# Attention beside a Fourier mix on one core: the place of a unit's negated maximum, the columns of the value matmuls, and two smaller edits

## The chip, the cores and the metric

The kernel runs on one core of one Trainium2 chip. The metric is the device time of one execution in microseconds (us), the median of several runs. All matrices are float32; TensorE reads most of them in the float32r form.

## The reference

The input x has 2048 rows of 640. Two branches are computed from it and mixed by a gate per row:

```python
q, k, v = split(x @ wqkv)                       # 32 heads of 20
p = softmax(q @ k.T * 20**-0.5)                 # 2048 x 2048 for each head
a = (p @ v, heads side by side) @ wo            # 640 x 640
b = dft_seq_re @ (x @ dft_hid_re.T) - dft_seq_im @ (x @ dft_hid_im.T)
g = sigmoid((x * gate_w).sum(-1))
out = g * a + (1 - g) * b
```

## The kernel before

Heads are taken in 16 pairs, and each pair in two halves of the queries, so attention has 32 **units** of 1024 queries by 2048 keys for two heads. PE computes the scores of a unit twice. The first time (`s_mm`, kind "m") queries lie on the output rows, and DVE takes the maximum of every 512 keys (L199) as soon as the scores stand in PSUM. The second time (kind "e", L950) keys lie on the output rows, with the negated maximum added through two extra rows of the query stack, and ACT takes the exponential (L952) into the tile `p`. The maximum work runs 41 steps ahead of the exponentials (`LEAD`); a unit is 32 steps, each with two "m" and two "e" matmuls.

When the last maximum of a unit is done, `max_nm` reduces its 128x64 block maxima to 128x16 negated ones on DVE (`nm`, L213). `max_chain` transposes them on PE (L231), splits the transpose in two on DVE (L115, L116) and sends the rows to the query stack by DMA.

The value product is `av_step`: for one key tile of 128 keys four matmuls (two heads, two query blocks), each with its own strip of 32 output rows of one PSUM bank `av`. The stationary operand is a piece of `v`, the tile of a pair's values, in which a head has 21 columns (20 values and a column of ones that gives the softmax's sum). A piece of 32 columns reaches into the next head's columns, and past the end for the last one, for which `v` has 16 more columns, set to zero on POOL. In the trace each of these float32 matmuls counts as two.

Under the attention runs the Fourier branch, piece by piece: first the products with the hidden matrices (`hid_tile`, L379), then seven products with sums of sequence matrices (`dft_step`, L636), last the output projection (`out_tile`, L743). The sequence matrices come by DMA as `raw` tiles (three buffers in turn), are combined on POOL (L516), cast on ACT (L113), and the rest is split off on POOL (L116) into a `part` tile (two buffers). In the seventh product `dft_step` also loads the five row blocks of the output weights `wo` through `raw` tiles, and POOL splits each in four instructions.

The order of all this is written out by hand. A string in `ORDERS` gives, for one **cycle**, the order of "e" and "m" scores, of fills "F" with Fourier matmuls, and at its end a burst "B": the value matmuls of the key tiles that are done, three of them in the Fourier stage (`k == 1`) and two elsewhere. There, too, the burst holds the unit's `max_nm` and, ahead of its last key tile, `max_chain`. Instructions stand on each engine in the order in which they are called. Score tiles share five PSUM banks in turn (`bank`), so a score matmul waits until the reader of the score five before it is done.

Ahead of all this the projections of q and k (`qk_tile`) run with weights in `part` tiles: the rounded part and the rest of 640 columns each, made by `w_tiles`, 4096 bytes apart. The values' projection (`v_pair`) gathers its results in `v` tiles.

Of the kernel before, what the change touches and what calls it, by code (L numbers as in the profile page):

```python
# [11 lines left out]
F32 = mybir.dt.float32  # L12
# [7 lines left out]
P = 128  # L20
# [3 lines left out]
DH = 20  # L24
ND = D // P
NS = S // P
NP = H // 2
HE = D // 2
VW = 2 * (DH + 1)
# [48 lines left out]
def mix_kernel(ctx: ExitStack, tc: tile.TileContext, xa, wqk, wb, cdft, wo, out):  # L78
# [59 lines left out]
    def part_tile():  # L138
        return work.tile([P, 2, 1024], R, name="part", bufs=2)

    def w_tiles():
        w = part_tile()
        return [w[:, z, : ND * P].rearrange("p (d c) -> p d c", d=ND) for z in range(2)]

    def v_tile():
        return work.tile([P, NS * VW + 16], F32, name="v", bufs=2)

# [27 lines left out]
        p, u = VISITS[n]  # L177
        return third["q"] if p == 14 else qst[place(p)][:, u * (S // 2) : (u + 1) * (S // 2)]

    mx, nms, ends = {}, {}, []  # L180
    now, later = [-1], {}

    def at_step(i, fn):
# [17 lines left out]
    def s_end(i):  # L201
        n, s = divmod(i, 32)
        if n < NU and s == 31:
            if now[0] < 0:
                max_nm(n)
            else:
                ends.append(n)
        if s == 1 and 0 < n <= NU and now[0] < 0:
            max_chain(n - 1)

    def max_nm(n):
        nms[n] = small.tile([P, 16], F32, name="nm", bufs=2)
        dve.tensor_reduce(nms[n], mx.pop(n).rearrange("p h q c -> p (h q) c"), axis=AX.X, op=ALU.max, negate=True)  # L213
# [47 lines left out]
    vts = {}  # L261

    def load_v(n):
        p = VISITS[n][0]
        if n and VISITS[n - 1][0] == p:
            vts[n] = vts[n - 1]
            return
        vts[n] = v_tile()
        pool.memset(vts[n][:, NS * VW :], 0.0)
        sp.dma_start(vts[n][:, : NS * VW].rearrange("p (s e) -> p s e", s=NS), v_scr[p])  # L270

    def load_x(t):
        for d in range(0, ND, 2):
# [75 lines left out]
            three(ps[:, :n], x[:, 0, d, cs], x[:, 1, d, cs], w[:, 0, d, :n], w[:, 1, d, :n], d == 0, d == ND - 1)  # L349

    def v_pair(hf, s):
        vst = v_tile()[:, : NS * VW].rearrange("p (a k e) -> p a k e", a=NP // 2, k=2)
        pool.memset(vst, 1.0)
        for k in range(2):
            ps = bank()
            mm_b(hf, s + k, ps, HE + 2 * hf)
            act.activation(
                vst[:, :, k, :].rearrange("p a (h e) -> p a h e", h=2)[:, :, :, :DH],
                ps[:, :HE].rearrange("p (a h e) -> p a h e", h=2, e=DH), AF.Copy)
            if hf:  # L360
                act.activation(logit[:, s + k : s + k + 1], ps[:, HE : HE + 1], AF.Copy)
        stores.append((
            v_scr[hf * (NP // 2) : (hf + 1) * (NP // 2), :, s : s + 2, :].rearrange("a p k e -> p a (k e)"),
            vst.rearrange("p a k e -> p a (k e)")))
        flush(1)
# [181 lines left out]
    def av_step(i, n, kt, split_unit):  # L547
        v = vts[n]
        if split_unit:
            next_av()  # L550
        t, c0 = av["tile"], kt * VW
        pp = [pts.pop((n, kt, qc)) for qc in range(2)]
        for qc in range(2):
            for h in range(2):
                j = 2 * qc + h
                pe.matmul(t[32 * j : 32 * j + 32, :], v[:, c0 + h * (DH + 1) : c0 + h * (DH + 1) + 32],  # L556
                          pp[qc][:, h, :], start=kt == 0, stop=kt == NS - 1)
        if kt == NS - 1:
            unit_end(i, n)

# [52 lines left out]
    def dft_step(g):  # L613
        n, t, s = g // NS // HT, g // NS % HT, g % NS
        if s == 0:
            new_y(0), new_y(1)
            outs[n, t] = []
        if s % 8 == 0 and g // 8 + 3 < 2 * UNITS:
            cfin.append(load_c(g // 8 + 3))
        if s % 8 == 2 and g // 8 + 2 < 2 * UNITS:  # L620
            cfin[0][0]()
        if s == 8:
            for _, th, hf in PRODUCTS[n][2]:
                tt = th * HT + t
                y = None
                if (tt, hf) in signs:
                    y = apool[0].tile([P, HE], F32, name="yt", bufs=4)
                    sp.dma_start(y, y_scr[tt, :, hf * HE : (hf + 1) * HE])
                outs[n, t].append(y)
        c = cparts[g // 8]  # L630
        cs = slice((s % 8) * P, (s % 8 + 1) * P)
        a = at[n % 2, s]
        for z, (cz, az) in enumerate(((0, 0), (0, 1), (1, 0))):
            for h in range(2):
                r = slice(64 * h, 64 * h + 64)
                pe.matmul(yp[h][:, :HE], c[r, cz, cs], a[r, az], start=s == 0 and z == 0, stop=s == NS - 1 and z == 2)  # L636
            if z < 2:
                yield
        w = g % (HT * NS) - 16
        if n + 1 == len(PRODUCTS) and w >= 0:  # L640
            d, r = divmod(w, 8)
            if r == 0 and d < ND:
                wos[d] = raw_tile()[:, :D]
                sp.dma_start(wos[d], wo[:, d])
            if r == 5 and d < ND:
                raw = wos.pop(d)
                for h in range(2):
                    wos[d, h] = a_tile(1, 2 * d + h)
                    split(wos[d, h][:, 0], wos[d, h][:, 1], raw[:, h * HE : (h + 1) * HE], pool, pool)
        if s == NS - 1:  # L650
            m = apool[1].tile([P, HE], F32, name="m", bufs=2)
            y0, y1 = yp[0][:, :HE], yp[1][:, :HE]

            def read():
                act.activation(m, y0, AF.Copy)
                dve.tensor_tensor(m, y1, m, op=ALU.add)

            extras.append((now[0], read))
            for out_, y in zip(PRODUCTS[n][2], outs.pop((n, t))):
                extras.append((now[0] + 3, functools.partial(finish_y, out_, t, m, y)))  # L660
        yield
# [163 lines left out]
    start = 4 * HID  # L825
# [129 lines left out]

    def burst(c):
        for n in ends:
            max_nm(n)
        k, _, i = phase(c)
        steps = 6 if k == 1 else 4  # L960
        run_extras(steps - 2)
        if k == 1:
            run_casts()
        for kt in range(i // 2, (i + steps) // 2):
            if k == 1 and ends and kt == (i + steps) // 2 - 1:
                max_chain(ends.pop(0))
            av_step(now[0], kt // NS, kt % NS, kt % NS == 0 and kt > i // 2)
        while ends:
            max_chain(ends.pop(0))
        if c in (HID - NS - 1, HID - 1):  # L970
            next_pool()
# [4 lines left out]
    for c in range(len(goals)):  # L976
        k, base, i = phase(c)
        order, *heads_ = ORDERS[k]
        first = dict(zip("em", heads_))
        for x, kind in enumerate(order):  # L980
            if kind == "F":
                fill(c)
            elif kind == "B":
                burst(c)
            else:
                score(kind)
            if k == 1 and x == len(order) // 2:
                run_loads(c - HID)
# [114 lines left out]
```

## Time and profile before

| | |
|---|---|
| runs | 1876.40, 1879.57 and 1880.56 us; median 1879.57 |
| the profiled execution | 1879.31 us; its span 1877.5 us, mean granted clock 0.998 |
| PE, PE's weight loads, DVE, ACT, POOL busy | 99%, 73%, 74%, 72%, 53% of the span |
| value matmuls (L556) | 4096, 485.3 us busy |
| negated maxima (L213) and their transposes (L231) | 32 of each; 6.8 and 8.9 us busy |

A row of the timeline or of a group names the line, the engine and the operation, then output and inputs by the program's names, then shapes; PEld is PE's weight load, which runs beside matmuls. In square brackets stands how long the engine had been empty before the row, and whose end it waited for last. Rows of the waits give total us, times and the longest. A matmul's own duration overlaps with its neighbours', so what counts on PE is the distance between starts.

### The profile page before, as it was taken

Reading aid. Unit: us, or ns where it says so; the run is one execution under the profiler, and the core shown is the slowest. Engines: PE = TensorE matmul, PEld = TensorE weight load, DVE = VectorE, ACT = ScalarE, POOL = GpSimd, SP = SyncE. Lnnn points to the kernel's source line nnn. Section 1 sums busy time; section 2 is a strip of 40 time slices with the busy share of each in tenths; the row PEclk is TensorE's granted clock in tenths of the full one; section 3 lists DMA queues with packets and bytes.
Section 4 is the critical chain, followed back from the end, with each engine's and each line's share of the span. In section 5 each row is a group of like instructions: output and inputs, shape, how many; then the busy total and the mean of one; then the engine's idle time right before and its main releaser. Section 6 shows DMA issues by size and latency. Waiting matters only on the chain.

```text
span 1877.5 us, 44813 instructions
## 1 busy us (share of the span) xinstructions
PE 1858.4 (99%) x17606; PEld 1372.2 (73%) x17606; DVE 1380.5 (74%) x2309; ACT 1355.7 (72%) x2645; POOL 1002.0 (53%) x851
## 2 busy tenths in 40 slices
PE   9999999999999999999999999999999999999998
PEld 8988777676767777777777777777777777776666
DVE  3043457887877888888888888888888888888853
ACT  4222257787877787788788788778878877778885
POOL 3334432121146676344678688655668767545544
PEclk9999999999999999999999999999999999999999
DMA  6754341222134673536567576646375856531233
GB/s 228 164 146 148 136 129 55 78 64 68 53 102 135 211 217 127 155 116 192 183 191 232 162 248 198 186 136 182 127 231 186 244 174 194 172 90 52 83 97 108
DMA packets 178771, 281.61 MB, mean 150 GB/s; under 512 B 44811, under 2 KB 113547, under 8 KB 178559
## 3 DMA queue, kind: packets, MB, share of 16 engines
q1 hardware_dynamic: 177599, 276.77, 48.4%
q0 software_dynamic: 960, 1.97, 0.6%
q8 instruction: 138, 2.26, 0.5%
q14 instruction: 74, 0.61, 0.1%
HBM read 214.61 MB, written 63.52 MB: 148 GB/s over the span
## 4 chain that ended last, share of the span: by engine, by line
PE 95%; DVE 3%; issue 0%; DMA 0%; POOL 0%; ACT 0%; SPq 0%; POOLq 0%; ACTq 0%; DVEq 0%
PE ps L556 23%; PE yp L636 19%; PE ps L950 17%; PE ps L197 14%; PE yp L379 7%; PE ps L119 4%; PE ps L120 4%; PE ps L121 4%; PE yp L743 3%; DVE mx L199 3%; PE ps L231 0%; DMA p<-in_xa 0%; DVE nm L213 0%; PE ps L1037 0%; POOL raw L516 0%
## 5 line engine op out<-in xcount | busy, mean ns | idle before, releaser
L199 DVE TENSOR_REDUCE mx<-ps 128x1 f32<-128x512 f32 x2048 | 1280.7, 683 | 327.7 <-PE ps L197 297.5
L952 ACT ACTIVATE p<-ps 128x512 f32<-128x512 f32 x2048 | 1054.1, 611 | 298.9 <-PE ps L197 193.8
L950 PE MATMUL ps<-qst,kst 62*128 62x512 f32 x1920 | 728.2, 407 | 0.1
L197 PE MATMUL ps<-kst,qst 60*128 60x512 f32 x1920 | 668.1, 411 | 0.0
L636 PE MATMUL yp<-x,part 64*128 64x320 f32 x5376 | 629.2, 307 | 0.0
L636 PEld LDWEIGHTS yp<-x,part 64*128 64x128 f32 x5376 | 606.0, 186 | 5.8 <-ACT raw L389 0.4
L556 PE MATMUL ps<-p,v 128*32 128x512 f32 x4096 | 485.3, 597 | 0.0
L116 POOL TENSOR_TENSOR part<-raw,part 128x1024 fp32r<-128x1024 f32 (+1 forms) x128 | 287.2, 2244 | 345.2 <-ACT part L113 329.5
L950 PEld LDWEIGHTS ps<-qst,kst 62*128 62x128 f32 x1920 | 341.7, 185 | 155.0 <-DVE mx L199 85.5
L197 PEld LDWEIGHTS ps<-kst,qst 60*128 60x128 f32 x1920 | 318.7, 184 | 12.5 <-issue 4.2
L556 PEld LDWEIGHTS ps<-p,v 128*32 128x32 f32 x4096 | 110.8, 109 | 233.0 <-issue 225.1
L379 PE MATMUL yp<-wb,x 64*128 64x320 f32 x1920 | 224.5, 307 | 0.0
L379 PEld LDWEIGHTS yp<-wb,x 64*128 64x128 f32 x1920 | 210.1, 186 | 6.4
L390 POOL TENSOR_TENSOR raw<-raw 128x320 f32<-128x320 f32 x64 | 55.7, 870 | 268.1 <-ACT raw L389 215.0
L516 POOL TENSOR_TENSOR raw<-raw,raw 128x1024 f32<-128x1024 f32 x77 | 185.2, 2405 | 0.1
L113 ACT ACTIVATE part<-raw 128x1024 fp32r<-128x1024 f32 (+2 forms) x121 | 123.4, 1020 | 6.0 <-POOL raw L516 4.1
L743 PE MATMUL yp<-x,part 64*128 64x320 f32 x768 | 102.6, 309 | 0.0
L339 ACT ACTIVATE p<-ps 128x512 f32<-128x512 f32 x40 | 23.8, 597 | 104.1 <-PE ps L121 101.1
L116 POOL TENSOR_TENSOR x<-araw,x 128x320 fp32r<-128x320 f32 x112 | 97.9, 882 | 1.3
L743 PEld LDWEIGHTS yp<-x,part 64*128 64x128 f32 x768 | 92.0, 186 | 1.0
L119 PE MATMUL ps<-x,part 128*128 128x512 f32 x200 | 81.4, 407 | 1.5 <-ACT x L113 1.3
L120 PE MATMUL ps<-x,part 128*128 128x512 f32 x200 | 80.0, 400 | 0.2 <-DVE x L116 0.2
(102 smaller groups left out, 1363.1 us busy)
## 6 DMA issues: line engine op xcount, KB each, us to landing
raw<-in_cdft SPq DMA_DIRECT2D x192, 512.0 KB
araw<-a_scr SPq DMA_DIRECT2D x192, 160.0 KB
qk_scr<-p SPq DMA_DIRECT2D x40, 512.0 KB
kst<-qk_scr SPq DMA_DIRECT2D x84, 160.0 KB
qst<-qk_scr SPq DMA_DIRECT2D x84, 160.0 KB
yt<-y_scr SPq DMA_DIRECT2D x80, 160.0 KB
a_scr<-raw SPq DMA_DIRECT2D x64, 160.0 KB
y_scr<-yt SPq DMA_DIRECT2D x64, 160.0 KB
```

Source lines behind the costliest of these rows:

```text
L116: e2.tensor_tensor(dst2, src, f32(dst1), op=ALU.subtract)
L119: pe.matmul(ps, st1, mv1, start=first, stop=False)
L120: pe.matmul(ps, st1, mv2, start=False, stop=False)
L197: pe.matmul(ps, q[b : b + KROWS, qt * P : (qt + 1) * P], k[b : b + KROWS, kc * 512 : (kc + 1) * 512], start=True, stop=True)
L199: return lambda: dve.tensor_reduce(mx[n][:, h, qt, kc : kc + 1], ps, axis=AX.X, op=ALU.max)
L379: pe.matmul(yp[h][:, :HE], x[r, xz, d, cs], w[r, wz, d, :HE], start=d == 0 and z == 0, stop=d == ND - 1 and z == 2)
L516: pool.tensor_tensor(raws[0], raws[0], raws[1], op=ALU.add if PRODUCTS[n][0][1][0] > 0 else ALU.subtract)
L556: pe.matmul(t[32 * j : 32 * j + 32, :], v[:, c0 + h * (DH + 1) : c0 + h * (DH + 1) + 32], pp[qc][:, h, :], start=kt == 0, stop=kt == NS - 1)
L636: pe.matmul(yp[h][:, :HE], c[r, cz, cs], a[r, az], start=s == 0 and z == 0, stop=s == NS - 1 and z == 2)
L743: pe.matmul(yp[h][:, :HE], o[oz][r], wos[d, hf][r, wz], start=d == 0 and z == 0, stop=end)
L950: pe.matmul(pt, k[b : b + KROWS + 2, kt * P : (kt + 1) * P], q[b : b + KROWS + 2, qc * 512 : (qc + 1) * 512], start=True, stop=True)
L952: act.activation(pts[n, kt, qc][:, h], pt, AF.Exp, scale=float(DH) ** -0.5)
```

## The change

Four things change. `max_nm` is called right behind a unit's last maximum in the Fourier stage, and the burst calls it only where that has not been done. The value matmuls take 21 columns for all key tiles but a unit's first, which keeps 32 so that the whole strip is written once; with it the pad of `v` and its memset go. `w_tiles` lays the two parts one behind the other, 2560 bytes apart. The output weights' loads and splits come every 16 steps of the seventh product in place of every 8.

```diff
     def w_tiles():
-        w = part_tile()
-        return [w[:, z, : ND * P].rearrange("p (d c) -> p d c", d=ND) for z in range(2)]
+        w = part_tile().rearrange("p z c -> p (z c)")[:, : 2 * ND * P].rearrange("p (z d c) -> p z d c", z=2, d=ND)
+        return [w[:, z] for z in range(2)]
 
     def v_tile():
-        return work.tile([P, NS * VW + 16], F32, name="v", bufs=2)
+        return work.tile([P, NS * VW], F32, name="v", bufs=2)
...
             if now[0] < 0:
                 max_nm(n)
             else:
+                if early:
+                    max_nm(n)
                 ends.append(n)
...
         vts[n] = v_tile()
-        pool.memset(vts[n][:, NS * VW :], 0.0)
-        sp.dma_start(vts[n][:, : NS * VW].rearrange("p (s e) -> p s e", s=NS), v_scr[p])
+        sp.dma_start(vts[n].rearrange("p (s e) -> p s e", s=NS), v_scr[p])
...
                 j = 2 * qc + h
-                pe.matmul(t[32 * j : 32 * j + 32, :], v[:, c0 + h * (DH + 1) : c0 + h * (DH + 1) + 32],
-                          pp[qc][:, h, :], start=kt == 0, stop=kt == NS - 1)
+                r, m = c0 + h * (DH + 1), DH + 1 if kt else 32
+                pe.matmul(t[32 * j : 32 * j + m, :], v[:, r : r + m], pp[qc][:, h, :], start=kt == 0, stop=kt == NS - 1)
...
         if n + 1 == len(PRODUCTS) and w >= 0:
-            d, r = divmod(w, 8)
+            d, r = divmod(w, 16)
...
     def burst(c):
         for n in ends:
-            max_nm(n)
+            if n not in nms:
+                max_nm(n)
...
         first = dict(zip("em", heads_))
+        early[:] = [c] if k == 1 else []
```

PE and ACT keep their order instruction for instruction. On DVE 14 of the 32 reductions `nm` move. The first place is the end of the Fourier stage's first cycle with a unit's end in it; `mx_7821` holds that unit's maxima, `mx_8697` the next unit's, and `ps0` to `ps5` are the banks. Before:

```order
L199 TENSOR_REDUCE mx_7821<-ps0_8667 128x1
L199 TENSOR_REDUCE mx_7821<-ps2_8677 128x1
L199 TENSOR_REDUCE mx_8697<-ps4_8698 128x1
L199 TENSOR_REDUCE mx_8697<-ps0_8701 128x1
L199 TENSOR_REDUCE mx_8697<-ps2_8707 128x1
L199 TENSOR_REDUCE mx_8697<-ps3_8710 128x1
L213 TENSOR_REDUCE nm_8713<-mx_7821 128x16
```

And now (the numbers of the tiles differ from build to build):

```order
L199 TENSOR_REDUCE mx_7817<-ps0_8662 128x1
L199 TENSOR_REDUCE mx_7817<-ps2_8672 128x1
L215 TENSOR_REDUCE nm_8675<-mx_7817 128x16
L199 TENSOR_REDUCE mx_8694<-ps4_8695 128x1
L199 TENSOR_REDUCE mx_8694<-ps0_8698 128x1
L199 TENSOR_REDUCE mx_8694<-ps2_8704 128x1
L199 TENSOR_REDUCE mx_8694<-ps3_8707 128x1
```

The reduction moves ahead of four maxima of the next unit; so it does in seven units. In seven others the unit's last maximum comes earlier in its cycle. DVE before, two units on, where `mx_9579` is the unit's:

```order
L199 TENSOR_REDUCE mx_9579<-ps1_10433 128x1
L199 TENSOR_REDUCE mx_10443<-ps5_10444 128x1
L199 TENSOR_REDUCE mx_10443<-ps3_10455 128x1
L199 TENSOR_REDUCE mx_10443<-ps5_10474 128x1
L199 TENSOR_REDUCE mx_10443<-ps3_10484 128x1
L199 TENSOR_REDUCE mx_10443<-ps2_10503 128x1
L199 TENSOR_REDUCE mx_10443<-ps5_10506 128x1
L199 TENSOR_REDUCE mx_10443<-ps3_10512 128x1
L199 TENSOR_REDUCE mx_10443<-ps1_10515 128x1
L213 TENSOR_REDUCE nm_10518<-mx_9579 128x16
```

And now:

```order
L199 TENSOR_REDUCE mx_9574<-ps1_10427 128x1
L215 TENSOR_REDUCE nm_10430<-mx_9574 128x16
L199 TENSOR_REDUCE mx_10439<-ps5_10440 128x1
L199 TENSOR_REDUCE mx_10439<-ps3_10451 128x1
L199 TENSOR_REDUCE mx_10439<-ps5_10470 128x1
L199 TENSOR_REDUCE mx_10439<-ps3_10480 128x1
```

Here it moves ahead of eight, of which the first two free banks (`ps5`, `ps3`) that scores of the same cycle write again (`ps5_10474`, `ps3_10484` before).

On POOL the output weights' splits (L115 and L116 on `x` from `raw`) stand elsewhere in the seventh product. Before, from the end of a unit's normalisation (L588) to the fifth split:

```order
L588 TENSOR_TENSOR o<-o,rb 128x512
L115 CAST x_24259<-raw 128x320
L116 TENSOR_TENSOR x_24259<-raw,x_24259 128x320
L115 CAST x_24259<-raw 128x320
L116 TENSOR_TENSOR x_24259<-raw,x_24259 128x320
L116 TENSOR_TENSOR part<-raw,part 128x1024
L269 MEMSET v 128x16
L516 TENSOR_TENSOR raw<-raw,raw_24664 128x1024
L115 CAST x_23778<-raw 128x320
L116 TENSOR_TENSOR x_23778<-raw,x_23778 128x320
L115 CAST x_23778<-raw 128x320
L116 TENSOR_TENSOR x_23778<-raw,x_23778 128x320
```

And now:

```order
L589 TENSOR_TENSOR o<-o,rb 128x512
L116 TENSOR_TENSOR part<-raw,part 128x1024
L517 TENSOR_TENSOR raw<-raw,raw_24644 128x1024
L115 CAST x_24245<-raw 128x320
L116 TENSOR_TENSOR x_24245<-raw,x_24245 128x320
L115 CAST x_24245<-raw 128x320
L116 TENSOR_TENSOR x_24245<-raw,x_24245 128x320
```

The four instructions ahead of the subtraction into `part` are gone (they were the fourth split), and at the fifth's place stands the third one; the last two follow 16 and 32 steps later. On SP the loads of these two move with them.

More of the change, by code (lines that the diff above doesn't have):

```diff
@@ L178, in q_unit @@
         return third["q"] if p == 14 else qst[place(p)][:, u * (S // 2) : (u + 1) * (S // 2)]
-    mx, nms, ends = {}, {}, []
+    mx, nms, ends, early = {}, {}, [], []
     now, later = [-1], {}
@@ L351, in v_pair @@
     def v_pair(hf, s):
-        vst = v_tile()[:, : NS * VW].rearrange("p (a k e) -> p a k e", a=NP // 2, k=2)
+        vst = v_tile().rearrange("p (a k e) -> p a k e", a=NP // 2, k=2)
         pool.memset(vst, 1.0)
```

## The prediction

> **What bounds the kernel now.** I read the page first: the span, the engines' busy time and the chain that ended last.
>
> ```profile
> span 1877.5 us, 44813 instructions
> PE 1858.4 (99%) x17606; PEld 1372.2 (73%) x17606; DVE 1380.5 (74%) x2309; ACT 1355.7 (72%) x2645; POOL 1002.0 (53%) x851
> PE 95%; DVE 3%; issue 0%; DMA 0%; POOL 0%; ACT 0%; SPq 0%; POOLq 0%; ACTq 0%; DVEq 0%
> ```
>
> The end is set by PE. DVE, ACT and POOL have a quarter to a half of the span free, so an edit is worth what it takes out of PE's own row: a wait there, or a matmul that starts sooner. I therefore looked next in the waits for what stops PE's weight loads, and found one row that the change touches.
>
> ```profile
> PEld ps L231 <- DVE nm L213: 36.3, 31, 1.4
> ```
>
> L231 is the transpose of a unit's 16 negated maxima, L213 the reduction that makes them. Not all of the 36.3 us is a wait: a transpose never follows value matmuls at once. The timeline shows the floor, in the hidden-product stage, and then the same spot in the Fourier stage for the three kinds of unit there.
>
> ```profile
> 293.72 0.21 DVE L213 TENSOR_REDUCE nm<-mx 128x16 f32<-128x64 f32 x1
> 294.51 0.09 PEld L231 LDWEIGHTS ps<-ident,nm 128*16 128x16 f32 x1 [0.84 <-DVE nm L213]
> ...
> 640.88 2.48 DVE L199 TENSOR_REDUCE mx<-ps 128x1 f32<-128x512 f32 x4 [0.30 <-PE ps L197]
> 643.28 0.21 DVE L213 TENSOR_REDUCE nm<-mx 128x16 f32<-128x64 f32 x1
> 643.54 0.09 PEld L231 LDWEIGHTS ps<-ident,nm 128*16 128x16 f32 x1 [1.29 <-DVE nm L213]
> ...
> 688.46 2.48 DVE L199 TENSOR_REDUCE mx<-ps 128x1 f32<-128x512 f32 x4 [0.41 <-PE ps L197]
> 690.98 0.22 DVE L213 TENSOR_REDUCE nm<-mx 128x16 f32<-128x64 f32 x1
> 691.25 0.09 PEld L231 LDWEIGHTS ps<-ident,nm 128*16 128x16 f32 x1 [1.42 <-DVE nm L213]
> ...
> 748.21 0.09 PEld L231 LDWEIGHTS ps<-ident,nm 128*16 128x16 f32 x1 [1.30 <-DVE nm L213]
> ```
>
> At 294.51 the maxima were ready 0.58 us before (293.72 + 0.21), yet the load row is empty for 0.84 us: that is the floor, PE emptying itself of value matmuls. At 643.54, 691.25 and 748.21 the load starts 0.05 us after L213 ends: there PE really waits, 0.45, 0.58 and 0.46 us over the floor. The sum agrees: of the 31 waits ten are at the floor, 14 like 643.54 and seven like 691.25, 10 x 0.84 + 14 x 1.30 + 7 x 1.42 = 36.5.
>
> **The maxima's place.** In the order of DVE 14 of the 32 reductions stand earlier, all in the Fourier stage: seven by four maxima (the unit at 643.54 is the first) and seven by eight (the one at 748.21). For the seven units at 691.25 and its like nothing moves; their last maximum is itself the last of the cycle. With the reduction ahead of the four maxima that run from 640.88, the transpose no longer waits: 14 x 0.46 = 6.4 us. What is late next at this spot is the floor itself. After the burst nothing takes the wait over: DVE's L115 and L116 read the transpose, and only the first scores after the burst need DVE again, a full burst tail later.
>
> The reduction now delays the maxima behind it by its 0.21 us. For the four-step units it falls in DVE's idle 0.30 us ahead of 640.88, so it is free. For the eight-step units it stands inside a run of maxima:
>
> ```profile
> 741.94 1.29 DVE L199 TENSOR_REDUCE mx<-ps 128x1 f32<-128x512 f32 x2 [0.18 <-PE ps L197]
> 743.29 0.19 PEld L197 LDWEIGHTS ps<-kst,qst 60*128 60x128 f32 x1
> ```
>
> The first of these two maxima is the unit's last; the second ends at 743.23 and frees the bank that the load at 743.29 writes next, so that load was already waiting for DVE. Put 0.21 us between the two and PE's load is late by up to that. I charge 0.2 us to each of the seven: 6.4 - 1.4 = 5.0 us gained. Bounds: 6.4 if PE's other row half covers the delay, 3.6 if all 14 units pay it.
>
> **Value matmuls of 21 columns.** One part of the line view gives minimum, median and maximum:
>
> ```profile
> L556 PEld LDWEIGHTS ps<-p,v x4096: 105/110/111, 261.8 to 1858.6; 128*32 128x32 f32 x196
> L556 PE MATMUL ps<-p,v x4096: 592/592/618, 261.8 to 1859.0; 128*32 128x512 f32 x196
> ...
> 1003.48 0.16 PEld L556 LDWEIGHTS ps<-p,v 128*32 128x32 f32 x8 [0.29 <-issue]
> 1003.94 0.13 PEld L556 LDWEIGHTS ps<-p,v 128*32 128x32 f32 x4 [0.30 <-issue]
> 1004.37 0.13 PEld L556 LDWEIGHTS ps<-p,v 128*32 128x32 f32 x4 [0.30 <-issue]
> ```
>
> Four matmuls, one to each strip of 32 output rows, run side by side, and a group follows the last after 0.43 us (1004.37 - 1003.94). At a burst's start eight loads stand together: two groups' weights go in, and later loads run while matmuls stream. So a load is hidden, except the first of a burst: there matmuls show 618 in place of 592 ns, and the next group comes after 0.46 us. A load of 21 columns in place of 32 can only shorten that 25 ns, in proportion by 25 x 11 / 32 = 8.6 ns. By the code there are 200 bursts (56, 112 and 32); 18 begin with key tile 0, which keeps 32 columns, and 21 start again behind a transpose: 203 x 8.6 ns = 1.7 us. The streaming, 512 columns of p, does not change. Bounds: nothing, or 2.4 us if the draining at a burst's end shortens too, by 3 ns for each of 200.
>
> **Output weights.** Five loads and their splits on POOL come every 16 product steps, not every 8. Before, the fifth one cost PE something:
>
> ```profile
> 1576.91 0.88 POOL L116 TENSOR_TENSOR x<-raw,x 128x320 fp32r<-128x320 f32 x1
> 1579.09 2.40 POOL L116 TENSOR_TENSOR part<-raw,part 128x1024 fp32r<-128x1024 f32 x1
> 1581.52 0.33 SPq L644 DMA_DIRECT2D raw<-in_wo  x1
> 1588.09 0.46 POOL L115 CAST x<-raw 128x320 fp32r<-128x320 f32 x1 [4.21 <-DMA raw<-in_wo]
> 1594.01 2.38 POOL L516 TENSOR_TENSOR raw<-raw,raw 128x1024 f32<-128x1024 f32 x1
> 1596.42 1.06 ACT L113 ACTIVATE part<-raw 128x1024 fp32r<-128x1024 f32 x1 [3.23 <-POOL raw L516]
> 1598.02 0.50 PE L197 MATMUL ps<-x 60*128 60x512 f32 x1 [1.21 <-ACT p L952]
> ...
> 1574.81 1.06 ACT L113 ACTIVATE part<-raw 128x1024 fp32r<-128x1024 f32 x1 [0.49 <-POOL raw L516]
> 1615.51 2.38 POOL L116 TENSOR_TENSOR part<-raw,part 128x1024 fp32r<-128x1024 f32 x1 [5.90 <-ACT part L113]
> 1634.14 2.39 POOL L116 TENSOR_TENSOR part<-raw,part 128x1024 fp32r<-128x1024 f32 x1 [3.59 <-ACT part L113]
> ```
>
> POOL waits at 1588.09 for the load; the combination L516 behind it ends at 1596.39; ACT's cast waits 3.23 us for that, with the exponentials behind it, and PE 1.21 us for those. That load was issued at 1581.52, as the subtraction at 1579.09 ended and gave up one of three raw buffers; and the subtraction itself stood behind the fourth split. Now no split stands there, and with three buffers taken in turn a weight load every 16 steps always gets the one that the last weight load left. So the load leaves some 1.5 us earlier, ACT waits about 1.7 us, and PE, which lost nothing at an ACT wait of 0.49 (1574.81), loses little: 1.2 us gained. Sixteen steps take some 19 us (1615.51 to 1634.14), so two splits move to about 1607 and 1626, where POOL idles 5.90 and 3.59 us against their 2.7. Bounds: 1.2 gained, or the old stall kept and repeated at both new places, 2.4 lost.
>
> **The two edits with no price.** The memset of the pad, and the distance of the weights' parts:
>
> ```profile
> L269 POOL MEMSET v<- 128x16 f32 x19 | 2.2, 117 | 0.0
> L120 PEld LDWEIGHTS ps<-x,part 128*128 128x128 f32 x200 | 38.2, 191 | 9.0 <-DVE x L116 0.5
> L120 PEld LDWEIGHTS ps<-wb,x 128*128 128x128 f32 x160 | 30.2, 189 | 0.1
> ```
>
> The 2.2 us lie on POOL, which is 53% busy and not on the chain; without that cover it would still be 2.2. The weights at L120 sit in a tile with parts 4096 bytes apart; the other weights, in a tile with parts 6440 bytes apart, load in 189 against 191 ns. Spacing shows at most 2 ns on 600 loads, 1.2 us either way; I take nothing.
>
> **The sum.** 5.0 + 1.7 + 1.2 = 7.9 us against the profiled execution's 1879.31 (span 1877.5 and 1.8 around it; the runs' median, 1879.57, is the same within 0.3): 1871.4.
>
> **The rivals.** First, DVE gives the gain back: all 14 units pay 0.25 us (the reduction and the late start behind it), and neither the columns nor the output weights bring anything: 1879.3 - 2.9 = 1876.4. For it speaks the load at 743.29 with no slack; against it the 0.30 us idle at 640.88. 0.12.
>
> Second, the output weights stall ACT at both new places and still at the old one: 1879.3 - 5.0 - 1.7 + 2.4 = 1875.0. For it, POOL's 4.21 us wait for such a load; against it, POOL's idle time at the new places. 0.08.
>
> Third, going from 32 to 21 columns makes PE empty itself. A strip count that does not fill its strip can be seen in the rows already:
>
> ```profile
> 640.45 0.39 PE L197 MATMUL ps<-kst,qst 60*128 60x512 f32 x1
> 640.50 0.31 PE L636 MATMUL yp<-x,part 64*128 64x320 f32 x1
> 640.68 0.39 PE L950 MATMUL ps<-qst,kst 62*128 62x512 f32 x1
> ```
>
> Matmuls of 60, 64 and 62 rows follow each other within 0.05 to 0.18 us, without the hole that a change between value and score matmuls has. A change at each unit's second key tile would cost the burst-end drain, 0.1 us, and an open load, 0.02, 32 times: 3.8 us, 1875.2. 0.05. The Trainium skill (TensorEngine Tiling (Array Packing), Key Properties) says that changing the tiling mode, not just the tile, drains TensorE; whether an active-column count alone is a mode it doesn't say, and by the strict reading the sum would be 1875.2, by the loose one 1871.4. The three rows above agree with the loose one, for rows; for columns no row here shows it.
>
> Fourth, slower: loads that don't fill their strip are no longer taken in behind the running matmuls. Then each of the 1024 groups less the 221 that are open already pays 25 x 21 / 32 = 16 ns: 13 us, 1871.4 + 13 = 1884.4. It decides from 10 ns a group (7.9 us over 803). Against it: loads of 60 and 62 rows are taken in early as those of 64 are; for it: nothing here loads 21 columns. 0.06.
>
> **How the numbers follow.** The forecast has 0.69. Its own bounds are 6.4 + 2.4 + 1.2 + 1.2 at best, 1868, and about 3.6 alone at worst, 1876; runs of one kernel differ by 2 us from their median (1876.4 to 1880.56). The range 1867 to 1876.5 takes in the first three rivals and leaves out the fourth and some of each edge. What a measurement can tell from no change is about 0.2%, 3.8 us: faster means under 1875.8. That is nearly all of the forecast (0.66) and about half of the first three rivals (0.13); slower is the fourth and a little of the second.
>
> **What would show it.** Right: L231's load row loses about 6 us of waiting and the 14 moved units stand at 0.84; the seven others stay at 1.42; matmuls at L556 keep 592 ns, with a maximum near 609; no PE wait on ACT near 1598. Wrong: groups of value matmuls further apart than 0.43 us, a hole behind each key tile 0, or waits of PE on maxima in the cycles with an eight-step unit that add up to more than 1.4 us.

## The result, and the profile after

The changed kernel takes 1867.17 us, the median of four runs (1864.15 to 1869.01), against 1880.07 for four runs of the kernel before: ratio 0.9933, with a 95% interval from 0.9913 to 0.9952. That is 0.7% faster, and 4.2 us below the forecast of 1871.4, at the low edge of its range. The profiled run took 1869.01 us.

The page says that the same engine sets the end, with a little more on the chain that is not PE (DMA 4%, before 0%):

```profile
span 1867.2 us, 44796 instructions
PE 1850.2 (99%) x17606; PEld 1360.0 (73%) x17606; DVE 1380.7 (74%) x2309; ACT 1355.6 (73%) x2645; POOL 1003.8 (54%) x832
PE 93%; DMA 4%; DVE 1%; POOL 1%; SPq 0%; issue 0%; ACT 0%; POOLq 0%; ACTq 0%; DVEq 0%
```

All lines behind the first ones moved by one or two: the transpose of the maxima is now L233, `nm` L215, the value matmuls L558, ACT's exponentials L953.

The waits of PE's weight load at the transpose, as total us, times and longest. Before there was, beside the row of 36.3 us, one more:

```profile
PEld ps L231 <- DVE yt L759: 0.8, 1, 0.8
```

And now:

```profile
PEld ps L233 <- DVE nm L215: 18.4, 17, 1.5
PEld ps L233 <- DVE mx L199: 11.9, 14, 0.8
PEld ps L233 <- DVE yt L760: 0.8, 1, 0.8
```

Their sum fell from 37.1 to 31.1 us, by the 6 us that were forecast. The 14 units of the second row are the moved ones: 11.9 / 14 = 0.85 us, the floor. In the timeline, the three spots of the Fourier stage again, in the same order:

```profile
638.30 0.09 PEld L233 LDWEIGHTS ps<-ident,nm 128*16 128x16 f32 x1 [0.85 <-DVE mx L199]
...
685.59 0.22 DVE L215 TENSOR_REDUCE nm<-mx 128x16 f32<-128x64 f32 x1
685.86 0.09 PEld L233 LDWEIGHTS ps<-ident,nm 128*16 128x16 f32 x1 [1.44 <-DVE nm L215]
...
742.39 0.09 PEld L233 LDWEIGHTS ps<-ident,nm 128*16 128x16 f32 x1 [0.85 <-DVE mx L199]
```

The first and the third stood at 1.29 and 1.30 before; the second, whose last maximum is the cycle's last, still waits for `nm`.

The value matmuls, with minimum, median and maximum in ns:

```profile
L558 PEld LDWEIGHTS ps<-p,v x4096: 96/101/111, 258.0 to 1848.4; 128*21 128x21 f32 x183, 128*32 128x32 f32 x13
L558 PE MATMUL ps<-p,v x4096: 592/592/618, 258.0 to 1848.8; 128*21 128x512 f32 x183, 128*32 128x512 f32 x13
```

The matmul keeps its 592 ns; the 618 are the bursts that begin with a key tile 0 and its 32 columns. By the starts of successive matmuls a burst's second group now follows its first after 444.3 ns where the burst begins with 21 columns (453.4 before, and 453.2 now in the 18 bursts that begin with 32), and later groups follow after 429 as before.

The output weights did not do what was forecast. The third of their loads, its split on POOL, and what waits behind it:

```profile
1569.01 0.33 SPq L645 DMA_DIRECT2D raw<-in_wo  x1
1578.96 0.45 POOL L115 CAST x<-raw 128x320 fp32r<-128x320 f32 x1 [7.61 <-DMA raw<-in_wo]
1582.52 2.37 POOL L116 TENSOR_TENSOR part<-raw,part 128x1024 fp32r<-128x1024 f32 x1
1584.85 2.38 POOL L517 TENSOR_TENSOR raw<-raw,raw 128x1024 f32<-128x1024 f32 x1
1587.26 1.06 ACT L113 ACTIVATE part<-raw 128x1024 fp32r<-128x1024 f32 x1 [3.60 <-POOL raw L517]
1588.85 0.50 PE L197 MATMUL ps<-x 60*128 60x512 f32 x1 [1.62 <-ACT p L953]
```

It is the old chain, from POOL's wait for the load to PE's wait for ACT, a little longer than before (7.61 for 4.21, 3.60 for 3.23, 1.62 for 1.21 us). By the clock the load left 12.5 us earlier than the fifth one did before, and its split began 9.1 us earlier. But PE, too, was 9.6 us further on: its wait began at 1587.23 (1588.85 - 1.62), and at 1596.81 before. So against PE's own course the load left 2.9 us earlier, and the split began 0.45 us later. The stretches from 1540 to 1600 us show how busy the DMA engines were; after the clock stands their busy share, then GB/s:

```profile
1540.00:1569.00 29.00, 29.00 (x298) 21.12 (x296) 24.74 (x43) 22.83 (x45) 19.67 (x14) 1.00 0.54 168
1569.00:1579.00 10.00, 10.00 (x107) 7.49 (x105) 8.12 (x14) 7.75 (x16) 2.40 (x2) 1.00 0.84 227
1579.00:1600.00 21.00, 18.84 (x190) 13.18 (x189) 16.04 (x29) 13.77 (x27) 15.91 (x14) 1.00 0.55 174
```

While it was under way the DMA engines were at 84%, with loads of key and query stacks among their work. That alone does not explain the 10 us to the split, since before, where a load took 6.6, they were as busy:

```profile
1581.50:1588.10 6.60, 6.60 (x70) 4.23 (x68) 5.11 (x9) 4.45 (x9) 2.40 (x3) 1.00 0.82 266
```

What the load waited for is not shown.

A wait that this profile has and the one before hardly shows is DVE's for the softmax sums, which come back from memory:

```profile
1175.08 0.35 SPq L576 DMA_DIRECT2D lc<-l_scr  x1
1183.61 0.25 DVE L579 RECIPROCAL lc<-lc 128x16 f32<-128x16 f32 x1 [1.74 <-DMA yt<-y_scr]
1184.46 0.50 PE L197 MATMUL ps<-kst,qst 60*128 60x512 f32 x1 [1.44 <-DVE mx L199]
```

`lc` was asked for 8.5 us before the reciprocal could run (the transfer named last, of `yt`, is not its input); the maxima queued behind it on DVE, and PE waited 1.44 us. Such waits of PE come at one or another cycle in some of the profiles below, up to 1.83 us at one place, and in others not at all.

### The profile page after: what moved, and what is told of

It reads as the page before. It is cut to its first block, busy times and chain, and to the rows that moved or that the text cites. A ratio compares the mean times of both kernels' runs of the same rounds, so it can differ in the third digit from the quotient of the medians.

```text
span 1867.2 us, 44796 instructions
## 1 busy us (share of the span) xinstructions
PE 1850.2 (99%) x17606; PEld 1360.0 (73%) x17606; DVE 1380.7 (74%) x2309; ACT 1355.6 (73%) x2645; POOL 1003.8 (54%) x832
## 4 chain that ended last, share of the span: by engine, by line
PE 93%; DMA 4%; DVE 1%; POOL 1%; SPq 0%; issue 0%; ACT 0%; POOLq 0%; ACTq 0%; DVEq 0%
PE ps L558 23%; PE yp L637 18%; PE ps L951 16%; PE ps L197 13%; PE yp L380 7%; PE ps L119 4%; PE ps L121 4%; PE ps L120 4%; PE yp L744 3%; DVE mx L199 1%; DMA kst<-qk_scr 1%; DMA lc<-l_scr 1%; DMA raw<-in_wo 1%; DMA raw<-in_cdft 0%; POOL part L116 0%; PE ps L233 0%
## 5 line engine op out<-in xcount | busy, mean ns | idle before, releaser
L953 ACT ACTIVATE p<-ps 128x512 f32<-128x512 f32 x2048 | 1054.3, 613 | 292.6 <-PE ps L197 167.4
L951 PE MATMUL ps<-qst,kst 62*128 62x512 f32 x1920 | 725.9, 406 | 0.1
L197 PE MATMUL ps<-kst,qst 60*128 60x512 f32 x1920 | 668.3, 411 | 1.6 <-DVE mx L199 1.6
L558 PE MATMUL ps<-p,v 128*21 128x512 f32 (+1 forms) x4096 | 483.3, 596 | 0.0
L116 POOL TENSOR_TENSOR part<-raw,part 128x1024 fp32r<-128x1024 f32 (+1 forms) x128 | 287.3, 2244 | 331.2 <-ACT part L113 307.5
L951 PEld LDWEIGHTS ps<-qst,kst 62*128 62x128 f32 x1920 | 341.3, 185 | 156.4 <-DVE mx L199 86.4
L197 PEld LDWEIGHTS ps<-kst,qst 60*128 60x128 f32 x1920 | 320.0, 184 | 15.0 <-issue 4.2
L558 PEld LDWEIGHTS ps<-p,v 128*21 128x21 f32 (+1 forms) x4096 | 101.7, 100 | 236.5 <-issue 226.8
L517 POOL TENSOR_TENSOR raw<-raw,raw 128x1024 f32<-128x1024 f32 x77 | 187.5, 2435 | 0.4 <-DMA raw<-in_cdft 0.4
L116 POOL TENSOR_TENSOR x<-araw,x 128x320 fp32r<-128x320 f32 x112 | 97.5, 877 | 1.3
```

The costliest lines, as they stand in the source:

```text
L116: e2.tensor_tensor(dst2, src, f32(dst1), op=ALU.subtract)
L197: pe.matmul(ps, q[b : b + KROWS, qt * P : (qt + 1) * P], k[b : b + KROWS, kc * 512 : (kc + 1) * 512], start=True, stop=True)
L517: pool.tensor_tensor(raws[0], raws[0], raws[1], op=ALU.add if PRODUCTS[n][0][1][0] > 0 else ALU.subtract)
L558: pe.matmul(t[32 * j : 32 * j + m, :], v[:, r : r + m], pp[qc][:, h, :], start=kt == 0, stop=kt == NS - 1)
L951: pe.matmul(pt, k[b : b + KROWS + 2, kt * P : (kt + 1) * P], q[b : b + KROWS + 2, qc * 512 : (qc + 1) * 512], start=True, stop=True)
L953: act.activation(pts[n, kt, qc][:, h], pt, AF.Exp, scale=float(DH) ** -0.5)
```

## The experiments

Each kernel is the kernel before with the edit shown, where nothing else is said. Times are medians, ratios are to the kernel before on the same chip. Two things are also worked out from the starts of matmuls in each profile: the distance of successive 512-column projection matmuls, and the length of the Fourier stage from the 9th to the 29th transpose, less what distances of over 0.45 us from a Fourier matmul to a score hold beyond 0.08 us each (the usual distance). The second is good to about 1 us: kernels that should agree in it differ by that much. Four of these profiles (only_wo_16, gap_before_k, end_transpose and end_and_distance) hold, in this stage, 3.41 us at half the granted clock; what that costs (under only_wo_16) is still in the column.

| kernel | time us | ratio [95%] | projections ns | Fourier stage us |
|---|---|---|---|---|
| before | 1880.07 | | 233.2 | 1017.7 |
| after | 1867.17 | 0.9933 [0.9913, 0.9952] | 229.4 | 1010.9 |
| only_spacing | 1880.97 | 1.0008 [0.9998, 1.0019] | 233.3 | 1017.3 |
| only_early_max | 1874.58 | 0.9981 [0.9972, 0.9989] | 233.2 | 1013.4 |
| only_21_columns | 1873.59 | 0.9964 [0.9951, 0.9976] | 229.4 | 1015.0 |
| only_wo_16 | 1880.85 | 1.0002 [0.9993, 1.0012] | 233.3 | 1019.1 |
| columns_pad_kept | 1878.71 | 0.9995 [0.9983, 1.0008] | 233.3 | 1017.0 |
| gap_before_x | 1874.91 | 0.9982 [0.9970, 0.9993] | 229.3 | 1016.2 |
| gap_before_k | 1878.73 | 0.9998 [0.9986, 1.0009] | 233.3 | 1018.6 |
| distance_0 | 1872.73, one run | | 227.5 | 1016.3 |
| distance_128 | 1880.92, one run | | 232.5 | 1019.4 |
| late_split | 1866.82 | 0.9936 [0.9920, 0.9953] | 229.2 | 1010.4 |
| end_transpose | 1866.58 | 0.9923 [0.9903, 0.9944] | 229.6 | 1009.9 |
| end_and_distance | 1865.97 | 0.9919 [0.9904, 0.9933] | 227.5 | 1009.1 |

### One part at a time

**only_spacing**: the weights' two parts 2560 bytes apart, alone.

```diff
-        w = part_tile()
-        return [w[:, z, : ND * P].rearrange("p (d c) -> p d c", d=ND) for z in range(2)]
+        w = part_tile().rearrange("p z c -> p (z c)")[:, : 2 * ND * P].rearrange("p (z d c) -> p z d c", z=2, d=ND)
+        return [w[:, z] for z in range(2)]
```

> Only the distance of the projection weights' two parts changes, 4096 to 2560 bytes. After the whole change the first transpose came 3.3 us earlier and the projections' matmuls at L119 to L121 followed each other after 229 in place of 233 ns on average. Theory (the distance does it): about 3.5 us less, the first transpose about 3.3 us earlier, matmul distance 229 ns. Rival (it is the shifted addresses of all later tiles, since the value tile lost its pad): no change, distance 233 ns. The prediction's own step: 0, at most 1.2 us.

It brings nothing: the projections keep 233 ns, and the interval ends at a gain of 0.4 us (0.0002 x 1880).

**only_early_max**: `max_nm` behind the last maximum, alone.

```diff
             else:
+                if early:
+                    max_nm(n)
                 ends.append(n)
...
-            max_nm(n)
+            if n not in nms:
+                max_nm(n)
...
+        early[:] = [c] if k == 1 else []
```

> Only the early call of the negated maximum. Theory: 14 transposes start at the floor of 0.52 us behind the last value matmul in place of 0.97, 0.46 us each, and the seven eight-step units give 0.2 back in the cycle before: 5.0 us less. Rival (PE's other row half covers that delay): 6.4 us less. Rival (all 14 pay): 2.9 to 3.6 us less.

The time falls by 3.6 us (0.0019 x 1879; 2.1 to 5.3), the Fourier stage by 4.3. The waits at the transpose are those of the kernel after:

```profile
PEld ps L233 <- DVE nm L215: 18.2, 17, 1.5
PEld ps L233 <- DVE mx L199: 11.7, 14, 0.8
```

**only_21_columns**: 21 columns, and `v` without its pad and memset, as in the change.

```diff
-        return work.tile([P, NS * VW + 16], F32, name="v", bufs=2)
+        return work.tile([P, NS * VW], F32, name="v", bufs=2)
...
-        pool.memset(vts[n][:, NS * VW :], 0.0)
...
-                pe.matmul(t[32 * j : 32 * j + 32, :], v[:, c0 + h * (DH + 1) : c0 + h * (DH + 1) + 32],
-                          pp[qc][:, h, :], start=kt == 0, stop=kt == NS - 1)
+                r, m = c0 + h * (DH + 1), DH + 1 if kt else 32
+                pe.matmul(t[32 * j : 32 * j + m, :], v[:, r : r + m], pp[qc][:, h, :], start=kt == 0, stop=kt == NS - 1)
```

> Only the value matmuls of 21 columns, with the pad of the value tile and its memset gone. Theory: the first group of a burst takes 445 in place of 453 ns and nothing else changes, 1.7 us less in all. Rival (the shifted addresses speed up the projections): 5 us less, with the first transpose 3.3 us earlier. Rival (a change of the active columns drains PE): 2 us more.

It brings 6.8 us (4.5 to 9.2), four times the forecast for the columns, and the projections, which know no value column, run at 229.4 ns. So something beside the columns is at work.

**only_wo_16**: the output weights every 16 steps, alone.

```diff
-            d, r = divmod(w, 8)
+            d, r = divmod(w, 16)
```

> Only the output weights one in 16 steps. The prediction's step: PE's wait of 1.2 us on ACT near 1598 us goes, 1.2 us less. Rival (the load lands late at that step whenever it is issued, because the query and key stacks of the last pair are loaded then): the wait stays, 0 to 0.5 us more, no new wait at the two later places.

No difference: 0.4 us slower, from 1.3 faster to 2.3 slower. POOL again waits for a load and PE for ACT:

```profile
1578.08 0.33 SPq L644 DMA_DIRECT2D raw<-in_wo  x1
1588.85 0.45 POOL L115 CAST x<-raw 128x320 fp32r<-128x320 f32 x1 [8.40 <-DMA raw<-in_wo]
1598.76 0.79 PE L197 MATMUL ps<-x 60*128 60x512 f32 x1 [2.30 <-ACT p L952]
```

PE's wait began at 1596.46, 0.35 us ahead of the kernel before. Against PE's course the load left 3.1 us earlier and the split began 1.1 us later: the load lands late whenever it is issued, as the rival has it. The long wait also had a price of its own. Here are the 3.4 us behind it, and those behind the wait of 1.62 us in the kernel after (the matmuls are the first number in brackets, the granted clock the third number from the end):

```profile
1598.75:1602.10 3.35, 3.35 (x22) 3.35 (x24) 1.68 (x3) 2.72 (x5) 3.35 (x2) 0.50 0.92 301
1588.90:1592.30 3.40, 3.40 (x38) 3.33 (x40) 2.77 (x6) 3.40 (x8) 3.40 (x2) 1.00 0.73 227
```

The clock stood at half for 3.41 us, and 16 matmuls fewer ran: an estimate of 16 x 3.40 / 38 = 1.4 us lost. The other three profiles named above have the same stretch, each within 1.5 us of the end of PE's longest wait (2.03, 1.83 and 1.79 us). Behind waits of 1.62 us and less no profile has one. With 1.4 us taken off, only_wo_16 (1017.7) and gap_before_k (1017.2) stand by the kernel before in the last column.

The four parts alone add up to -3.6 - 6.8 + 0.4 + 1.5 = -8.5 us, all together -12.6 (9.0 to 16.4). With half widths of 3.9 (the four, added as squares) and 3.7 us the two do not contradict each other; the profiles' Fourier stage adds up better: -4.3 for the maximum and -2.7 for columns with pad make -7.0, after less before is -6.8.

### What the missing pad does

The pad is two buffers of 64 bytes in each partition, and the tiles placed behind `v` move by 128 bytes without it, the rounded rows `x0` to `x3` among them. In the projections x moves and `part` is stationary. From the first `part` tile to `x0` lie, by the sizes in the code, two `part` tiles (16384 bytes), seven `p` (28672), two `v` (5504 before, 5376 after) and the pool `att` (6208): 56768 bytes before and 56640 after. The tiles' own steps (8192 bytes for `part`, 20480 for x, 4096 or 2560 for the two parts) are all multiples of 256, so all of them keep the same distance modulo 256: 192 before, 64 after.

**columns_pad_kept**: 21 columns, the pad and its memset left in place.

```diff
-                pe.matmul(t[32 * j : 32 * j + 32, :], v[:, c0 + h * (DH + 1) : c0 + h * (DH + 1) + 32],
-                          pp[qc][:, h, :], start=kt == 0, stop=kt == NS - 1)
+                r, m = c0 + h * (DH + 1), DH + 1 if kt else 32
+                pe.matmul(t[32 * j : 32 * j + m, :], v[:, r : r + m], pp[qc][:, h, :], start=kt == 0, stop=kt == NS - 1)
```

> Value matmuls of 21 columns, but the value tile keeps its pad and its memset, so that no later tile changes its address. Theory (the columns are worth only the shorter open loads, the rest of the 5.7 to 6.8 us came from addresses): 1.7 us less, the first group of a burst at 445 ns, the projections' matmuls at 233 ns. Rival (the columns themselves are worth it all): 5.7 us or more less, projections at 229 ns.

The projections are back at 233.3 ns, and of the 6.8 us 0.9 are left (from 3.2 faster to 1.5 slower): the columns' own share, for which 1.7 was forecast.

```profile
L557 PE MATMUL ps<-p,v x4096: 592/592/617, 261.0 to 1855.8; 128*21 128x512 f32 x183, 128*32 128x512 f32 x13
```

The first two groups of its bursts stand 444.2 ns apart where they begin with 21 columns, as in the kernel after.

**gap_before_x** and **gap_before_k**: the kernel before with 128 unused bytes, once ahead of x alone (as `big`), once ahead of the key stacks (as `const`), so that `part` and x move together.

```diff
+    gap = big.tile([P, 32], F32, name="gap")
+    pool.memset(gap, 0.0)
     xs = [big.tile([P, 2, ND, 512], R, name=f"x{t}") for t in range(4)]
```

> The kernel before with a tile of 128 bytes ahead of the x tiles, set to zero once: x and the Fourier parts that take its place start at a multiple of 256 bytes, as after the change, where they stood 128 beside it. Nothing else moves but the first half's weights. Theory (the address of the moving operand sets the distance of the matmuls): projections at 229 in place of 233 ns, 4 to 5 us less in all. Rival (the pad's memset, or the smaller tile, did it): no change.

> The kernel before with the same 128 bytes ahead of the key and query stacks: these, which the scores' matmuls stream, come to a multiple of 256 bytes, and all later tiles but the right-hand side's with them, x too. Theory (it is the moving operand's address, for scores as well): 4 to 5 us less as with the gap before x, and up to 4 ns less for each of 4096 score matmuls, of which half run beside another: some 4 to 8 us more, 8 to 13 us less in all. Rival (it is something of the x tiles alone): as with the gap before x.

In both x begins 128 bytes further than before, at the same address. With the gap ahead of x alone the projections take 229.3 ns and the whole 3.4 us less (1.3 to 5.6); with `part` moved along, 233.3 ns and nothing. So x's own place does not decide; its distance to `part` does.

**distance_0** and **distance_128**: gaps of 64 and 192 bytes ahead of x, the other two distances.

```diff
+    gap = big.tile([P, 16], F32, name="gap")      # distance_128: 48
+    pool.memset(gap, 0.0)
```

> The kernel before, with 64 unused bytes ahead of the tiles x, so that the distance from the weights' part tile to x leaves 0 modulo 256 (192 in the kernel before, 64 in the kernel after). Read from the projections, whose matmuls of L119 to L121 follow each other after 233.2 ns in the kernel before and 229.3 ns after. Theory (the distance between the moving rows and the stationary tile decides): a value of its own, not bound to either. Rival (x itself must start at a multiple of 256 bytes; here it leaves 192): 233 ns.

> The kernel before, with 192 unused bytes ahead of the tiles x: the distance leaves 128 modulo 256, and x itself leaves 64. Theory (the distance decides): a value of its own; if 0 and 128 both give 229 or both give 233 ns, one residue alone is the bad or the good one. Rival (x itself must start at a multiple of 256 bytes): 233 ns here as well as at distance 0.

The projections' timeline, two rows of each kernel between which 18 matmuls start (before: 125.40 - 121.20, 4.20 us):

```profile
121.20 0.40 PE L120 MATMUL ps<-x,part 128*128 128x512 f32 x1
...
125.40 0.40 PE L120 MATMUL ps<-x,part 128*128 128x512 f32 x1
```

distance_0 (4.08 us):

```profile
120.25 0.39 PE L120 MATMUL ps<-x,part 128*128 128x512 f32 x1
...
124.33 0.39 PE L120 MATMUL ps<-x,part 128*128 128x512 f32 x1
```

distance_128 (4.17 us):

```profile
121.04 0.39 PE L120 MATMUL ps<-x,part 128*128 128x512 f32 x1
...
125.21 0.40 PE L120 MATMUL ps<-x,part 128*128 128x512 f32 x1
```

After, at distance 64 (4.12 us):

```profile
121.12 0.39 PE L120 MATMUL ps<-x,part 128*128 128x512 f32 x1
...
125.24 0.39 PE L120 MATMUL ps<-x,part 128*128 128x512 f32 x1
```

Over some 560 pairs of matmuls in each profile this makes 227.5, 229.4, 232.5 and 233.2 ns at 0, 64, 128 and 192: the distance has a value of its own at each residue, which the rival (x must begin at a multiple of 256) cannot give, since at distance 0 x is off such a multiple and the matmuls are fastest. The granted clock was 1.00 over the projections in all of these profiles, so it plays no part. The times of distance_0 and distance_128 come from one run each; the distances of the matmuls rest on the profiles.

### What could be had beside it

**late_split**: the kernel after, with the output weights' split eight steps later behind its load.

```diff
-            if r == 5 and d < ND:
+            if r == 13 and d < ND:
```

> The changed kernel, with the output weights' split 13 steps behind their load in place of 5. Theory (POOL stood waiting for the load, with the sequence matrices' work behind it): PE's wait on ACT of about 1.6 us near 1588 goes, 1.4 us less than the changed kernel, about 1865.5 us. Rival (the combination is late for its own load): the wait stays.

```profile
1567.63 0.33 SPq L645 DMA_DIRECT2D raw<-in_wo  x1
1576.84 2.45 POOL L517 TENSOR_TENSOR raw<-raw,raw 128x1024 f32<-128x1024 f32 x1
1579.20 0.48 POOL L115 CAST x<-raw 128x320 fp32r<-128x320 f32 x1
```

The split now runs 11.6 us after the load's issue and behind the combination L517, without a wait; ACT and PE do not wait there in this profile. In the two profiles below that share this edit they don't either, and in the eleven without it PE waits for ACT here, from 0.33 to 2.30 us. The times (1866.82 against 1867.17) are too close to tell apart, so the stall's price is shown in the profiles alone.

**end_transpose**: late_split with `nm` back in the burst and the transpose behind the whole burst.

```diff
-            if k == 1 and ends and kt == (i + steps) // 2 - 1:
-                max_chain(ends.pop(0))
...
-        early[:] = [c] if k == 1 else []
```

> The kernel after with output weights at r == 13, the reduction nm back in the burst, and the transpose of the maxima behind the whole burst of value matmuls in the Fourier stage, not ahead of its last key tile. Theory (what the transpose costs at its old place is the change from value matmuls to it and back, and a wait for nm where there is one): 21 units save 0.54 us of change each, 11.3 us, seven of them their remaining wait of 0.58 us, 4.1 us, and the reduction no longer delays maxima, 1.5 us: 17 us less than the kernel after, about 1850 us. Rival (the transpose behind the burst meets the next cycle's scores, and DVE's two splits L115 and L116 then hold up the next maxima, about 0.5 us a unit, or the change is paid there just the same): 1863 to 1868 us.

1866.58: the rival's range, far from 1850. All 21 transposes are at the floor, also the seven that waited, but the gain is gone by the next cycle. Part of it never was: a transpose inside the burst takes the place of a distance of 0.43 us between two groups, which the expectation left out. The distances from value matmuls to value matmuls, transposes and scores fell by 6.2 us over the stage. What followed the bursts gave most of that back:

```profile
742.53 0.09 PEld L233 LDWEIGHTS ps<-ident,nm 128*16 128x16 f32 x1 [0.85 <-DVE nm L215]
742.85 0.28 DVE L115 CAST m<-ps 16x128 fp32r<-16x128 f32 x1 [0.73 <-PE ps L233]
743.16 0.28 DVE L116 TENSOR_TENSOR m<-ps,m 16x128 fp32r<-16x128 f32 x1
743.37 1.27 DVE L199 TENSOR_REDUCE mx<-ps 128x1 f32<-128x512 f32 x2
743.50 0.18 PEld L951 LDWEIGHTS ps<-qst,kst 62*128 62x128 f32 x1 [0.46 <-DVE m L116]
```

DVE splits the transpose while the next cycle's first scores already wait in PSUM for their maxima, and the score at 743.50 waits for DVE. Over the stage the distances from a score of L197 to one of L951 rose by 7.6 us, and those the other way fell by 2.5. The stage without its longer waits is 0.5 us shorter than late_split's, or some 2 us with the half clock's 1.4 us taken off as well, not 17.

**end_and_distance**: late_split, the transpose behind the burst only for the seven units that no maximum follows, and 192 bytes ahead of x (distance 0).

```diff
+    gap = big.tile([P, 48], F32, name="gap")
+    pool.memset(gap, 0.0)
...
-            if k == 1 and ends and kt == (i + steps) // 2 - 1:
+            if k == 1 and ends and not fresh and kt == (i + steps) // 2 - 1:
```

(`fresh` holds a unit from its `max_nm` until the next maximum is called.)

> The kernel after with output weights at r == 13, the transpose behind the burst for the seven units alone whose reduction still holds PE up, and 192 unused bytes ahead of the tiles x, so that the distance from part to x leaves 0 modulo 256 in place of 64. Theory: the seven units lose their wait of 0.60 us and get back the 0.4 us that the first scores after the burst then wait for DVE, with 0.1 us less change, 2 us in all; the projections' matmuls follow each other after 227.5 in place of 229.3 ns, 0.9 us there and as much again in the other stages: 3.5 to 4 us less than the kernel with the late split alone (1866.8 us), about 1863 us. Rival (the distance decides nothing once the columns are 21, or the transpose's wait only changes its place): 1866 to 1867 us, with projections still at 229 ns or first scores that wait 0.6 us more.

Both steps show in the profile: 227.5 ns, and all seven transposes at 0.52 us behind the last value matmul in place of 1.12. The median, 1865.97, is the lowest, but it misses the forecast of 1863 and is not told apart from late_split's. The profile also holds a long wait for the softmax sums, with the stretch at half clock behind it:

```profile
1069.59 0.35 SPq L580 DMA_DIRECT2D lc<-l_scr  x1
1079.59 0.25 DVE L583 RECIPROCAL lc<-lc 128x16 f32<-128x16 f32 x1 [2.08 <-DMA lc<-l_scr]
1080.44 0.49 PE L198 MATMUL ps<-kst,qst 60*128 60x512 f32 x1 [1.79 <-DVE mx L200]
```

## Why the prediction was right, and where not

**The maxima's place** (5.0 us forecast) came out as worked out. By the starts of matmuls each of the 14 moved units stands 0.46 us nearer to its last value matmul, and in the seven eight-step units the cycle's scores ahead of the burst take 0.22 us more: 14 x 0.46 - 7 x 0.22 = 4.9. The part alone measured 3.6 (2.1 to 5.3). The seven others stayed, at 1.44.

**Value matmuls of 21 columns** (1.7 us forecast): 9.1 ns a burst against 8.6, so 203 x 9.1 ns = 1.8 us by the profile, and 0.9, within 1.5 slower to 3.2 faster, by the part alone. There is no drain: from the first matmul of a key tile 0, with 32 columns, to the first of key tile 1, with 21, it takes 882 ns at a burst's start and 858 further on, in both kernels, wherever the two stand in one burst. The strict reading of the Trainium skill (TensorEngine Tiling (Array Packing), Key Properties), under which a change of tiling mode drains TensorE, would have put the drain there; fewer active columns in the same strip are no such change here.

**Output weights** (1.2 us forecast) was wrong. The step that failed is that a load which leaves earlier also lands earlier, and so cuts ACT's wait by half. Against PE's course the load left 2.9 us earlier, twice the 1.5 forecast, but the split began 0.45 us later, and PE waited 1.62 us in place of 1.21; in only_wo_16 it was 3.1 us earlier, 1.1 later and 2.30. Over all eleven profiles with the split five steps behind its load, the load's issue spreads over 3.7 us of PE's course and the split's start over 2.0, and an earlier issue does not go with an earlier start. Why it lands when it does stays open. The price, too, was one value of many: in the nine profiles with the old spacing PE's wait runs from 0.33 to 2.03 us. The alternative in the bounds, the stall repeated at the two new places, did not come: POOL waits there, but ACT and PE do not. late_split shows what removes the stall: not an earlier load but a later reader.

**The two edits with no price** held only in part. The spacing is worth nothing, as said. The memset's own worth is not shown apart from its pad, but the pad had one: 128 bytes in the placement of tiles, which bring 3.4 us with the memset still in place. Of the memset's term only the POOL time was priced; that the tiles behind the pad move was not thought of. The size: 6.8 - 0.9 = 5.9 us as the difference of two parts, 3.4 (1.3 to 5.6) by the gap alone. In its profile some 1080 successive matmuls of all the projections follow each other after 190.9 in place of 192.6 ns on average, 1.8 us; the rest lies in the stages behind, where the Fourier stage of gap_before_x is 1.5 us shorter, near the limit of what that measure tells. Why it is that much there was not taken apart further: x, `part` and the other moved tiles all take part in those matmuls.

The maximum's 4.9, the columns' 1.8 and the gap's 3.4 give 10.1 us; with the 6.8 that columns and pad brought together it is 11.7, against 12.6 (9.0 to 16.4) measured. The forecast's 7.9 was short by the pad, and held 1.2 for the output weights that did not come. So the direction and the largest term were worked out, but that the time still lies in the range, by 0.2 us, is luck: the bounds had no term for the pad.

**The rivals.** None of the four happened. The loads stay hidden (592 ns, groups at 429), DVE gave back 1.5 us and no more, and PE's wait for output weights stayed single.

The Trainium skill (TensorE: Matmul & The Clock Gate, Step-by-step: what each phase is for) says that the streamed operand and the weight load have independent SBUF read ports, so that a load takes nothing from a running matmul. Here the distance between the two operands' addresses alone moves the matmuls from 227.5 to 233.2 ns, which that would not lead one to expect, and the measurement decides. Whether the two reads meet is not shown.

## What to carry to other kernels

An edit that changes the size of a tile also moves every tile placed behind it, so compare the addresses of operands before a gain is put down to the edit itself, and test it with a gap of unused bytes. A stall behind a load was cured here by a later reader and not by an earlier issue. When two profiles are compared in time, take off first by how much one kernel is ahead of the other at that place. A reduction that PE waits for belongs behind its last input, but only as far as the maxima that it delays have slack.

## What the runs showed of the hardware that was not expected

Projection matmuls (128x128 stationary, 512 moving columns, float32r) follow each other after 227.5, 229.4, 232.5 and 233.2 ns, as the moving tile's address less the stationary tile's leaves 0, 64, 128 and 192 modulo 256 bytes; distances of 56640 and 56896 bytes, 256 apart, gave 229.4 and 229.3. A moving tile at one and the same address gave 229.3 or 233.3, by where the weights were (gap_before_x and gap_before_k).

A weight load of 21 columns at a burst's start adds 15 ns to the distance of two groups (444.3 less 429.2) where one of 32 adds 24 (453.4 less 429.2), nearly in proportion to the columns; the loads behind running matmuls stay hidden at either width.

Behind a wait of PE of 1.79 us or more in the Fourier stage (four profiles) the granted clock stood at 0.50 for 3.41 us; in the other ten profiles, with waits of up to 1.62 us, it stayed at 1.00 in that stage. Where in between the limit lies, and whether it is the length alone, no run here shows.
